# Attention scores of 12 units made in the first six steps, kept in DRAM and fetched later

## Chip, core and metric

The kernel runs on one core of a Trainium2 chip. The metric is the device time of one execution in microseconds, the median of several runs. Engines are called as the profile calls them: PE (TensorE, matmuls), PEld (its weight loads), DVE (VectorE), ACT (ScalarE), POOL (GpSimd) and SP (SyncE, which here issues every DMA).

## What is computed

A top-k attention feeds a two-layer block. There are 8 batches of 8 heads, 576 positions and 64 dimensions a head; every row of scores keeps its 32 largest values.

```python
scores = (1 / sqrt(64)) * q @ k.T                    # 8 x 8 x 576 x 576
kth    = the 32nd largest of each row
scores = where(scores >= kth, scores, -1e9)
attn   = exp(scores - max); attn = attn / (sum(attn) + 1e-9)
x      = (attn @ v), heads side by side              # 4608 tokens x 512
h      = x @ w_in                                    # 512 -> 2048
out    = maximum(0.01 * h, h) @ w_out                # 2048 -> 512
```

All of it is float32.

## The kernel before

**Start.** Sixteen pieces of the weights are loaded and rounded (`round_weights`, L114), with the staging of raw bits in three `raw` buffers. Loads of q and k for the first head pairs, of v, and the scores of units 0 and 1 (`first_scores`, L229) stand between the last pieces (L501 to L517).

**Units and steps.** The attention is cut into 144 units. A whole unit is 128 query rows of one pair of heads, so 2 x 128 rows of 576 scores; a left unit joins the 64 remaining rows of two pairs. The main loop (L540) makes one step for each unit, and every step touches several units at once. At step s:

- DVE finds the top 32 of unit s (`top_k`, L244): a maximum and a minimum of the two halves of each row (L251), then four rounds of MAX8 (L256) with MATCH_REPLACE8 (L259) between.
- POOL masks unit s-1 (`mask`, L263), ACT takes its exponents (L273) and writes the sums to `ze` (L278).
- For unit s-2 DVE takes the reciprocal `rz` of `ze` (L282), ACT normalizes (L285) and splits the words into halves (`split`, L294), SP writes the halves to DRAM (`apart`, L295) and reads them back transposed as `wT` (L299). The units of HASTY are transposed on PE instead (L309, L315).
- PE weighs the values of two units together (`weigh_values`, L336). From unit 14 on this stands at the end of an even step, three steps after the odd unit of the two; the units of HURRIED come one step sooner. ACT copies the result to `x` (L350).
- At even s PE makes the scores of units s+2 and s+3 (`scores`, L203, matmuls L220), and ACT copies them from PSUM to `s_sb` (L227). `s_sb` has five buffers, taken in the order in which units are scored.

**The two layers.** Tokens are handled in 19 chunks: two of 128, then 17 of 256. A chunk is ready once its values are there. Its matmuls are L392 (first layer, `ph`, into `gT` by ACT at L398) and L404 (second layer, `pz`, copied by ACT at L413); the first two chunks go by L360, L365 and L377. They are cut into small pieces, which `mlp_steps` deals out over seven places in each step: `slot_budget` spreads the cost of what is ready until the next chunk will be ready. Scores and values do not count in that budget.

**What sets the order.** The program's order is written out by hand (`tc.manual_schedule`), and each engine goes through its own instructions in that order; an instruction that waits holds up all behind it on its engine. SP does the same with the DMAs. `load_more` (L489) loads v and q with k of later pairs at the end of a step. Eight pairs' q and k fit: five in `qt` and `kt`, three in the `raw` buffers that the weights no longer need.

```python
last = {p: n for n, u in enumerate(steps) for p in u.pairs}
while len(of) < NPAIR and (len(of) < n or last[len(of) - n] + lag <= s):
    load(len(of))
```

Of the kernel before, what the change touches and what calls it, by code (L numbers as in the profile page):

```python
# [9 lines left out]
F32 = mybir.dt.float32  # L10
# [10 lines left out]
def kernel(  # L21
# [41 lines left out]
    work = ctx.enter_context(tc.tile_pool(name="work", bufs=2))  # L63
    small = ctx.enter_context(tc.tile_pool(name="small", bufs=5))
    halves = ctx.enter_context(tc.tile_pool(name="halves", bufs=3, space=bass.MemoryType.DRAM))
    ps_sc = ctx.enter_context(tc.tile_pool(name="ps_sc", bufs=1, space=bass.MemoryType.PSUM))
    ps_ml = ctx.enter_context(tc.tile_pool(name="ps_ml", bufs=2, space=bass.MemoryType.PSUM))

# [31 lines left out]
    def load_weights(n):  # L100
        if n >= NPIECE:
            return
        if not AS_WORDS:
            nc.sync.dma_start(piece(n), weights[n])
            return
        raw_of[n] = raws.tile([P, WCH, 4], U16, name="raw")
        flat = raw_of[n].rearrange("p n w -> p (n w)")
        for m, c0, c1 in ROUNDED:
            if m == n:
                nc.sync.dma_start(flat[:, 4 * c0:4 * c1], weights[n][:, 4 * c0:4 * c1])  # L110
# [92 lines left out]
    def scores(us):  # L203


        narrow = ps_sc.tile([P, 2, 512], F32, name="narrow")
        ps = {}
        for k, u in enumerate(us):
            wide = ps_sc.tile([P, 2, 512], F32, name="wide", bufs=2)
            ps[u] = ((wide[:, :, 0:WIDE], 0, WIDE),  # L210
                     (narrow[:, :, k * NARROW:(k + 1) * NARROW], WIDE, S))

        order = ((us[0], 0), (us[0], 1), (us[1], 1), (us[1], 0))
        for u, part in order:
            to, k0, k1 = ps[u][part]
            for n in range(0, len(u.parts), 2):
                for i, pi, side, r0 in u.parts[n:n + 2]:
                    qt, kt = qk_of[pi]
                    d = slice(side * D, (side + 1) * D)
                    nc.tensor.matmul(to[r0:r0 + u.rows, i, :], qt[d, u.q0:u.q0 + u.rows],  # L220
                                     kt[d, k0:k1], start=True, stop=True)
        for u in us:
            u.both = work.tile([P, 2, S], F32, name="s_sb", bufs=5)
            u.s = [u.both[:, i, :] for i in range(2)]
        for u, part in order:
            to, k0, k1 = ps[u][part]
            nc.scalar.copy(u.both[:, :, k0:k1], to)  # L227

    def first_scores(u):  # L229

        ps = [ps_sc.tile([P, 2, 512], F32, name="wide", bufs=2) for i in range(2)]
        for half in range(2):
            for i, pi, side, r0 in u.parts:
                qt, kt = qk_of[pi]
                d = slice(side * D, (side + 1) * D)
                nc.tensor.matmul(ps[i][:, half, 0:HS], qt[d, u.q0:u.q0 + P],
                                 kt[d, half * HS:(half + 1) * HS], start=True, stop=True)
        yield
        u.both = work.tile([P, 2, S], F32, name="s_sb", bufs=5)
        u.s = [u.both[:, i, :] for i in range(2)]  # L240
        for i in range(2):
            nc.scalar.copy(u.s[i].rearrange("p (h n) -> p h n", h=2), ps[i][:, :, 0:HS])

    def top_k(u):  # L244

# [180 lines left out]
    def mlp_steps(budget):  # L426
        owed[0] += budget
        while owed[0] > 0:
            if running[0] is None:
                if not ready:  # L430
                    owed[0] = 0.0
                    return
                running[0] = mlp(ready.pop(0))
            cost = next(running[0], None)
            if cost is None:
                running[0] = None
            else:
                owed[0] -= cost
                backlog[0] -= cost
# [15 lines left out]

    steps = units

    def unit(n):
        return steps[n] if 0 <= n < len(steps) else None

# [25 lines left out]
    with tc.manual_schedule():  # L486
        last = {p: n for n, u in enumerate(steps) for p in u.pairs}

        def load_more(s):  # L489

            for of, load, n, lag in ((v_of, load_v, LOADED_V, LAG + 1), (qk_of, load_qk, LOADED + 3, 8)):
                while len(of) < NPAIR and (len(of) < n or last[len(of) - n] + lag <= s):
                    load(len(of))
                    if lag > LAG + 1 and len(of) > n:
                        break


        for n in range(3):
            load_weights(n)
        jobs = [round_weights(*job) for job in ROUNDED] if AS_WORDS else [iter(())] * len(ROUNDED)  # L500
        for n in range(len(jobs) + 1):  # L501
            if n == len(jobs) - 1:
                first = first_scores(steps[0])
                next(first, None)
            for job in jobs[max(n - 1, 0):n + 1][::-1]:
                next(job, None)
            if n == len(jobs) - 1:
                next(first, None)
                load_v(0)
                load_v(1)  # L510
            elif n == len(jobs):
                for _ in first_scores(steps[1]):
                    pass
            if n:
                load_weights(n + 2)
            if 0 <= n - len(jobs) + HP + 1 < HP:
                load_qk(n - len(jobs) + HP + 1)  # L517

        def weights_of(u):
            reciprocals(u)  # L520
            normalize(u, 0)
            normalize(u, 1)

        def values(*place):
            due = [u for n, u in enumerate(steps) if values_at(n) == place]
            if due:
                po = ps_sc.tile([P, 2, 512], F32, name="wide", bufs=2)[:, 0, 0:2 * P]
                po = po.rearrange("p (u n) -> p u n", u=2)
            else:
                return ()  # L530
            for n, u in enumerate(due):
                weigh_values(u, po[:, n, :])
            return [(u, po[:, n, :]) for n, u in enumerate(due)]

        def keep(weighed, *place):
            for u, po in weighed:
                keep_values(u, po)
            attended(*place)

        for s in range(len(steps) + LAG + 1):  # L540
            cur, old, older, new = unit(s), unit(s - 1), unit(s - 2), ()
            if s % 2 == 0:
                new = [u for u in steps[s + 2:s + 4] if u]
            picks = top_k(cur) if cur else iter(())
            budget = slot_budget(s)

            def slot():
                next(picks, None)

            at_first = s < HURRY and s - 2 in HURRIED  # L550
            if at_first:
                weights_of(older)
            slot()
            if old:
                mask(old, 0)
                mask(old, 1)
            late = s < HURRY and not {s - 1, s - 2} & set(HURRIED)
            if older and not late and not at_first:
                weights_of(older)
            mlp_steps(budget)  # L560
            weighed = values(s, MIDDLE)
            at_once = s - 2 in HURRIED or any(at == (s, MIDDLE) for at, _ in ready_at)
            if at_once:
                keep(weighed, s, MIDDLE)
            slot()
            if older and late:
                weights_of(older)
            if s - 2 in HASTY:
                transpose_in_haste(older)
            mlp_steps(budget)  # L570
            if old:
                exponents(old, 0)
            mlp_steps(budget)
            if older:
                keep_transposed(older) if s - 2 in HASTY else transpose(older, lambda: mlp_steps(budget))
            if not older or s - 2 in HASTY:
                mlp_steps(budget)
            slot()
            slot()
            mlp_steps(budget)  # L580
            if old:
                exponents(old, 1)
                sums(old)
            mlp_steps(budget)
            if not at_once:
                keep(weighed, s, MIDDLE)
            if new and s < HURRY:
                scores(new)
            keep(values(s, END), s, END)
            if new and s >= HURRY:  # L590
                scores(new)
            budget = slot_budget(s + 1)
            mlp_steps(budget)
            load_more(s)
        mlp_steps(1e9)

# [57 lines left out]
```

## Time and profile before

| what | value |
|---|---|
| median of 6 runs | 1468.27 us (1467.12 to 1468.9) |
| the profiled execution | 1468.9 us |
| its span, first to last instruction | 1467.1 us |
| granted TensorE clock, mean | 0.981 |
| start of step 0 (first L251) | 61.3 us |
| end of the last top-k | about 1381.4 us |
| DMA, all queues | 222.30 MB, mean 152 GB/s |
| DMA q1, share of 16 engines' span | 53.5% |
| apart, 288 KB, issue to landing | 2.1 us |
| kt, 288 KB, issue to landing | 3.7 us |
| wT, issue to landing | 4.6 us |

How to read what follows: in the page, a row of an engine is its busy time, its share of the span and its number of instructions. A row of 40 digits cuts the span in equal slices; a digit is the share in tenths (9 is 90% or more), and PEclk is the clock granted to TensorE. The chain is the work that ended last, followed back from the end, with each engine's share. In a table by stretch a row is start:end and length in us, then busy time and count of PE, PEld, DVE, ACT and POOL, the granted clock, the share of the DMA engines and GB/s. In a timeline a row is start, length, engine, line, operation, out<-in, and in brackets how long the engine had been idle and what ended that. Waits are listed as who waited for whom, with total us, times and longest. One execution is profiled; matmuls are pipelined, and their ends are modelled.

### The profile page before, as it was taken

What the parts mean: (1) busy time and instruction counts of PE and PEld (TensorE: products, weight loads), DVE (VectorE), ACT (ScalarE), POOL (GpSimd) and SP (SyncE); (2) the same over time, 40 slices, a digit from 0 to 9 for tenths busy, and PEclk for the clock granted to TensorE, in tenths of its full rate; (3) what the DMA queues carried; (4) which work ended last, traced back from release to release, by engine and by line L of the source; (5) the groups of instructions that cost most, each with busy time, mean ns of one, the idle gap of its engine ahead of it and who ended that gap; (6) DMA issues with size and microseconds to landing.
All of it is one profiled execution on the core that took longest, in us unless ns stands there. A gap on an engine that the chain in (4) does not pass through costs nothing.

```text
span 1467.1 us, 24106 instructions
## 1 busy us (share of the span) xinstructions
PE 1394.2 (95%) x8066; PEld 927.2 (63%) x8068; DVE 1320.4 (90%) x3401; ACT 1100.8 (75%) x1984; POOL 1096.6 (75%) x744
## 2 busy tenths in 40 slices
PE   7716999999999999999999999999999999999999
PEld 2314548575757676767676767666666666666674
DVE  7999999999999999999999999999999999999600
ACT  8758878777887777777777777777777777777710
POOL 3288888878888888787878788878787878787700
PEclk9958999999999999999999999999999999999999
DMA  9834534654366455664567445655457545554510
GB/s 329 303 85 134 145 105 116 171 153 136 108 196 183 130 138 153 171 185 137 146 166 199 136 137 137 189 171 151 127 160 208 139 136 139 161 139 135 144 49 14
DMA packets 388940, 222.30 MB, mean 152 GB/s; under 512 B 333904, under 2 KB 333904, under 8 KB 386896
## 3 DMA queue, kind: packets, MB, share of 16 engines
q1 hardware_dynamic: 388816, 220.77, 53.5%
q8 instruction: 63, 1.03, 0.3%
q14 instruction: 61, 0.50, 0.1%
HBM read 46.14 MB, written 92.01 MB: 94 GB/s over the span
## 4 chain that ended last, share of the span: by engine, by line
PE 79%; DVE 16%; DMA 2%; ACT 2%; issue 1%; SPq 0%; POOL 0%; DVEq 0%; ACTq 0%; POOLq 0%
PE pz L404 31%; PE ph L392 29%; PE wide L336 10%; DVE tops L256 7%; PE wide L220 6%; DVE pairs L259 5%; PE narrow L220 3%; DVE pairs L251 2%; DMA raw<-in_weights_dram 1%; DVE w_out L155 1%; DVE scale L152 0%; DMA wT<-apart 0%; DVE scale L131 0%; DVE top L133 0%; DMA vt<-in_vk_dram 0%
## 5 line engine op out<-in xcount | busy, mean ns | idle before, releaser
L269 POOL TENSOR_SCALAR pen<-s_sb,tops 128x576 f32<-128x576 f32 x288 | 637.5, 2213 | 210.5 <-DVE tops L256 145.4
L256 DVE MAX8 tops<-pairs 128x8 f32<-128x288 f32 (+1 forms) x1152 | 636.5, 592 | 0.0
L404 PE MATMUL pz<-w_out,gT 128*128 128x512 f32 x1152 | 505.5, 595 | 2.4 <-ACT scale L365 2.4
L392 PE MATMUL ph<-x,w_in 128*128 128x256 f32 x2176 | 482.9, 381 | 0.1
L259 DVE MATCH_REPLACE8 pairs<-tops,pairs 128x288 f32<-128x288 f32 (+1 forms) x864 | 460.6, 539 | 0.0
L392 PEld LDWEIGHTS ph<-x,w_in 128*128 128x128 f32 x2176 | 409.4, 190 | 76.9 <-issue 22.2
L270 POOL TENSOR_TENSOR s_sb<-s_sb,pen 128x576 f32<-128x576 f32 x288 | 406.6, 1412 | 24.1
L404 PEld LDWEIGHTS pz<-w_out,gT 128*128 128x128 f32 x1152 | 216.5, 190 | 267.2 <-issue 262.5
L294 ACT COPY split<-s_sb 128x1152 uint16<-128x1152 uint16 x280 | 309.4, 1146 | 0.0
L285 ACT ACTIVATE s_sb<-s_sb,rz 128x576 f32<-128x576 f32 x288 | 207.6, 773 | 42.6 <-DVE rz L282 42.6
L273 ACT ACTIVATE s_sb<-s_sb,nbias 128x576 f32<-128x576 f32 x288 | 222.3, 772 | 12.8 <-POOL s_sb L270 12.8
L251 DVE TENSOR_TENSOR pairs<-s_sb 128x576 f32<-128x576 f32 x288 | 213.5, 780 | 9.9
L336 PEld LDWEIGHTS wide<-wT,vt 128*64 128x64 f32 x3200 | 161.6, 139 | 68.0 <-issue 34.6
L336 PE MATMUL wide<-wT,vt 128*64 128x128 f32 (+1 forms) x3200 | 179.1, 268 | 25.5 <-ACT s_sb L227 21.8
L227 ACT COPY s_sb<-wide 128x704 f32<-128x704 f32 x142 | 107.1, 754 | 21.8 <-PE wide L220 21.8
L398 ACT ACTIVATE gT<-ph 128x512 f32<-128x512 f32 x136 | 80.7, 593 | 56.3 <-PE ph L392 55.6
L350 ACT COPY x<-wide 128x128 f32<-128x128 f32 (+1 forms) x160 | 32.2, 260 | 113.6 <-PE wide L336 113.6
L220 PE MATMUL wide<-kt,qt 64*128 64x352 f32 (+1 forms) x392 | 75.4, 498 | 26.2 <-ACT s_sb L227 23.0
L413 ACT COPY o_sb<-pz 128x512 f32<-128x512 f32 x36 | 21.1, 585 | 98.4 <-PE pz L404 98.4
L227 ACT COPY s_sb<-narrow 128x448 f32<-128x448 f32 x142 | 68.7, 536 | 0.8 <-PE narrow L220 0.2
L282 DVE RECIPROCAL rz<-ze 128x2 f32<-128x2 f32 x144 | 22.4, 155 | 47.3 <-ACT ze L278 47.2
L259 DVE MATCH_VALUE_LOAD pairs<-tops,pairs 128x8 f32 x864 | 63.4, 73 | 0.0
(61 smaller groups left out, 622.1 us busy)
## 6 DMA issues: line engine op xcount, KB each, us to landing
apart<-split SPq DMA_DIRECT2D x280, 288.0 KB, 2.1
raw<-in_weights_dram SPq DMA_DIRECT2D x15, 1024.0 KB, 7.1
vt<-in_vk_dram SPq DMA_DIRECT2D x32, 320.0 KB, 3.7
out_dram<-o_sb SPq DMA_DIRECT2D x36, 256.0 KB, 2.6
qt<-in_qT_dram SPq DMA_DIRECT2D x20, 288.0 KB, 3.2
kt<-in_kT_dram SPq DMA_DIRECT2D x20, 288.0 KB, 3.7
raw<-in_qT_dram SPq DMA_DIRECT2D x12, 288.0 KB, 3.4
raw<-in_kT_dram SPq DMA_DIRECT2D x12, 288.0 KB, 3.7
```

Source lines behind the costliest of these rows:

```text
L220: nc.tensor.matmul(to[r0:r0 + u.rows, i, :], qt[d, u.q0:u.q0 + u.rows], kt[d, k0:k1], start=True, stop=True)
L251: nc.vector.tensor_tensor(pairs[:, :, n, :], u.both[:, :, 0:HS], u.both[:, :, HS:S], op)
L256: nc.vector.max(out=u.tops[:, i, r, :], in_=rest[i])
L259: nc.vector.match_replace(out=rest[i], in_to_replace=u.tops[:, i, r, :], in_values=rest[i], imm_value=LOWEST)
L269: nc.gpsimd.tensor_scalar(pen, u.s[i], u.tops[:, i, ROUNDS - 1, 7:8], MASKED, ALU.is_lt, ALU.mult)
L270: nc.gpsimd.tensor_tensor(u.s[i], u.s[i], pen, ALU.add)
L273: nc.scalar.activation(u.s[i], u.s[i], AF.Exp, bias=u.nbias[:, i:i + 1], scale=SCALE, accum_out=u.z[:, i:i + 1])
L285: nc.scalar.activation(u.s[i], u.s[i], AF.Copy, bias=0.0, scale=u.rz[:, i:i + 1])
L294: nc.scalar.copy(split, pairs[:, :, h])
L336: nc.tensor.matmul(po[side * D:(side + 1) * D, o, :], vt[:, c, side, :], u.wT[:, c + side * NKC if c + 1 < NKC else c, r:r + n], start=(c ...
L392: nc.tensor.matmul(ph[:, i, 0:n], w_in[c][:, f * P:(f + 1) * P], x[c][:, 0:n], start=(c == 0), stop=(c == HP - 1),)
L404: nc.tensor.matmul(pz[0:m, 0:DMODEL], gT[:, f, r0:r0 + m], w_out[f // 4][:, f % 4, :], start=(f == 0), stop=(f == NFC - 1),)
```

## The change

Twelve whole units get their scores long before their step: 24, 25, 32, 33, then 40, 41, 48, 49, then 56, 57, 64, 65. Each group of four comes from two pairs of heads. While the weights' last pieces are rounded, `load_early` loads the two k and the four pieces of q of each group into one of the three `raw` buffers. At the end of steps 0 to 5, `score_early` makes the scores of 4, 2, 1, 2, 1 and 2 units: PE in two halves of 288 columns, ACT copies them into one of three places in `gT`, which holds no hidden layer yet, and SP writes 576 KB a unit to a DRAM tile of its own. Three steps before its own step, behind the transpose of the step, a unit's scores are fetched into an `s_sb` buffer. The scores of these six pairs at steps 22, 30, 38, 46, 54 and 62 are left out. Pairs 5 to 7 of q and k are loaded at the end of step 5 instead of step 0, as the `raw` buffers are taken until then. At one place HASTY stands for HURRIED.

```diff
+    def load_early(us):
+        raw = raws.tile([P, WCH, 4], U16, name="raw").rearrange("p n w -> p (n w)").bitcast(F32)
+        at = 0
+        for pi in sorted({u.pairs[0] for u in us}):
+            kt = raw[:, at:at + S]
+            nc.sync.dma_start(kt, kT[pi])
+            at += S
+            for u in us:
+                if u.pairs[0] == pi:
+                    early_of[u] = raw[:, at:at + P], kt
+                    nc.sync.dma_start(early_of[u][0], qT[pi][:, u.q0:u.q0 + P])
+                    at += P
+
+    def keep_scores(u):
+        k = len(kept_of)
+        qt, kt = early_of.pop(u)
+        ps = [ps_sc.tile([P, 2, 512], F32, name="wide", bufs=2) if (2 * k + i) % 3 else
+              ps_sc.tile([P, 2, 512], F32, name="narrow") for i in range(2)]
+        for half in range(2):
+            for i, _, side, _ in u.parts:
+                d = slice(side * D, (side + 1) * D)
+                nc.tensor.matmul(ps[i][:, half, 0:HS], qt[d, :], kt[d, half * HS:(half + 1) * HS],
+                                 start=True, stop=True)
+        both = gT.rearrange("p f n -> p (f n)")[:, k % 3 * 2 * S:(k % 3 + 1) * 2 * S]
+        for i in range(2):
+            nc.scalar.copy(both[:, i * S:(i + 1) * S].rearrange("p (h n) -> p h n", h=2), ps[i][:, :, 0:HS])
+        kept_of[u] = kept.tile([P, 2 * S], F32, name=f"kept{k}")
+        nc.sync.dma_start(kept_of[u], both)
+
+    def fetch_scores(u):
+        u.both = work.tile([P, 2, S], F32, name="s_sb", bufs=5)
+        u.s = [u.both[:, i, :] for i in range(2)]
+        nc.sync.dma_start(u.both.rearrange("p i n -> p (i n)"), kept_of[u])
...
+    KEPT = (24, 40, 56)
+    EARLY_SCORES = {0: 4, 1: 2, 2: 1, 3: 2, 4: 1, 5: 2}
...
+                if of is qk_of and to_keep:
+                    while len(of) < LOADED:
+                        load(len(of))
+                    continue
...
+            if n >= len(jobs) - 2:
+                load_early(to_load.pop(0))
             if 0 <= n - len(jobs) + HP + 1 < HP:
                 load_qk(n - len(jobs) + HP + 1)
...
-            at_once = s - 2 in HURRIED or any(at == (s, MIDDLE) for at, _ in ready_at)
+            at_once = s - 2 in HASTY or any(at == (s, MIDDLE) for at, _ in ready_at)
...
+            if unit(s + 3) in early_units:
+                fetch_scores(unit(s + 3))
             slot()
             slot()
...
+            if new and new[0] in early_units:
+                new = ()
             if new and s < HURRY:
                 scores(new)
             keep(values(s, END), s, END)
             if new and s >= HURRY:
                 scores(new)
+            score_early(EARLY_SCORES.get(s, 0))
```

## The prediction

> **What bounds the kernel now.** I read the page first: which engines are full, and which work the chain that ended last runs through.
>
> ```profile
> PE 1394.2 (95%) x8066; PEld 927.2 (63%) x8068; DVE 1320.4 (90%) x3401; ACT 1100.8 (75%) x1984; POOL 1096.6 (75%) x744
> ...
> PEclk9958999999999999999999999999999999999999
> ...
> PE 79%; DVE 16%; DMA 2%; ACT 2%; issue 1%; SPq 0%; POOL 0%; DVEq 0%; ACTq 0%; POOLq 0%
> ```
>
> Two engines are nearly full, and the chain changes between them, so an average says little. The chain in order of time is DVE from 61 to about 190 us, PE to about 375, DVE from 384 to 457, and PE from 463 to the end. I cut the span at starts of steps: L251 starts step 0 at 61.3 us, step 16 at 203.0, step 36 at 387.2 and step 48 at 493.6, and DVE's top-k is over at 1381.4. The table by stretch gives busy time of PE, PEld, DVE, ACT, POOL:
>
> ```profile
> 61.30:203.00 141.70, 90.04 (x519) 51.61 (x518) 140.52 (x368) 102.17 (x188) 112.99 (x77) 0.81 0.45 126
> 203.00:387.20 184.20, 183.11 (x1150) 125.22 (x1149) 176.38 (x460) 140.65 (x271) 149.66 (x101) 1.00 0.47 131
> 387.20:493.60 106.40, 105.21 (x620) 74.80 (x619) 105.55 (x277) 87.04 (x160) 89.81 (x61) 1.00 0.63 174
> 493.60:1381.40 887.80, 886.45 (x5318) 606.11 (x5317) 848.42 (x2208) 699.96 (x1284) 718.33 (x481) 1.00 0.57 154
> 1381.40:1467.10 85.70, 82.03 (x323) 49.97 (x322) 0.33 (x2) 17.21 (x30) 6.74 (x4) 1.00 0.18 51
> ```
>
> In the first stretch DVE is full and PE is idle for 51.7 us. In steps 36 to 47 twelve steps take 106.4 us, 8.87 each, with DVE full: that is DVE's floor, and PE is barely behind. In the second and fourth stretches PE is full and DVE is not. After 1381.4 only PE has work. The waits, asked for by stretch (221 to 387, 387 to 494, 494 to 1382; total, times, longest), show how the two are coupled:
>
> ```profile
> DVE rz L282 <- ACT ze L278: 6.2, 5, 2.5
> ```
> ```profile
> PE wide L336 <- DMA wT<-apart: 1.1, 2, 0.7
> ```
> ```profile
> DVE rz L282 <- ACT ze L278: 33.0, 39, 1.9
> ```
>
> Where PE is late, ACT waits in its fixed order for PE's scores and hidden layers, writes ze late, and DVE stalls at its reciprocal. Where DVE is the floor, PE waits for wT. So a PE microsecond is worth one where DVE still has stalls to give back (6.2 us in stretch two, 33.0 in four), and nothing in steps 36 to 44.
>
> **What is removed.** Six pairs of scores leave steps 22, 30, 38, 46, 54 and 62. One pair in PE's timeline:
>
> ```profile
> 268.29 0.86 PE L220 MATMUL wide<-kt,qt 64*128 64x352 f32 x4
> 268.99 0.54 PE L220 MATMUL narrow<-kt,qt 64*128 64x224 f32 x4
> 269.37 0.55 PE L220 MATMUL narrow<-raw 64*128 64x224 f32 x4
> 269.74 0.76 PE L220 MATMUL wide<-raw 64*128 64x352 f32 x4
> 270.43 0.70 PE L404 MATMUL pz<-w_out,gT 128*128 128x512 f32 x1
> ```
>
> From 268.29 to 270.43 is 2.14 us; the next work follows without a gap. Six pairs make 12.8 us. ACT also loses the pair's four copies (2 x 0.755 + 2 x 0.535 = 2.6 us), which only helps it to catch up. The order of all other instructions on PE, ACT, DVE and POOL is the same in both builds; the new tokens become ready at steps 42, 50, 58 and 66, so in the steps emptied PE goes straight on with hidden-layer work it already has.
>
> Now by stretch. Steps 22 and 30: 4.3 us; DVE's 20 steps there take 184.2 against a floor of 177.3, so 6.9 can be given back: it all passes. Step 38: PE already waits for wT at steps 40 and 42, so these 2.14 become more waiting: 0. Steps 46, 54, 62: 6.4 us. Eight steps take 73.8 us in steady state (L251 at 1141.4 and 1215.2), with one pair less 71.7, still over DVE's 70.9; so PE stays the bound, though with 0.8 us to spare. Counting 33.5 us from DVE's start of an odd unit to its landed wT (units 37 to 41, where nothing else delays it), wT would be there 1.3 us or more before PE at each even step from 48 to 68. Sum: 5 x 2.14 = 10.7 us.
>
> A rule of the Trainium skill speaks against this: "Perfetto Trace Analysis", section "Identifying the Most-Contended Engine", says that matmul occupancy is no measure of TensorE's headroom, and to use the busy share of the weight loads. By that, 63%, PE has a third to spare and the removal is worth nothing. The row says otherwise: from 494 to 1382 us PE waits 1.4 us for others. It is not at its peak rate, but its queue never empties, and a shorter queue ends sooner. I go by the row.
>
> **What is added early.** Twelve units at four matmul groups of 288 columns: 1.24 us each (L236), 14.9 us of PE. PE is idle for 38 of the 53 us of steps 0 to 5, and the granted clock there falls to 0.50. At half clock it is 30 us, which still fits. Value: 0 by either.
>
> ACT copies each unit in 1.17 us (L242, two copies). This must fit the gaps in which ACT waits for DVE's rz, the value before "<-DVE rz":
>
> ```profile
> 92.44 1.44 ACT L285 ACTIVATE s_sb<-s_sb,rz 128x576 f32<-128x576 f32 x2 [1.41 <-DVE rz L282]
> ...
> 101.30 1.44 ACT L285 ACTIVATE s_sb<-s_sb,rz 128x576 f32<-128x576 f32 x2 [3.56 <-DVE rz L282]
> ...
> 110.17 1.44 ACT L285 ACTIVATE s_sb<-s_sb,rz 128x576 f32<-128x576 f32 x2 [1.42 <-DVE rz L282]
> ```
>
> One unit follows each of steps 2 and 4 (gaps of 1.41 and 1.42) and two follow steps 1, 3 and 5 (gaps of 5.46, 3.56 and 3.24 against 2.34); the four after step 0 have 7.7 us. It fits. If it did not, DVE would still have some 3.5 us, as ze is written 97.54 to 97.74 and rz read at about 101.1. Queued behind the copies on ACT are normalize, exponents and splits, whose results are due two steps later. Between 0 and, with every copy twice as dear, 14 - 3.5 = 10 us; I take 0, as the copies are the same shape as L242.
>
> SP gets 18 loads at the start (2.5 MB), 12 writes of 576 KB, and six q and k loads moved from step 0 to step 5. Behind the first six loads stand qk of pair 3, due at 62 us, issued at 50.4 before: 0.85 MB at the 329 GB/s of the first slice is 2.6 us, so it lands by about 58. Behind the moved loads stands the apart of step 6, whose wT landed at 130.0 and is used at 145.1. Pairs 4 to 7 are first read at step 16. The staging in gT is free again by step 6; the first gT write (L377) is at 138.9. All 0 while DVE is the bound, up to step 16; uncovered, a few us at most.
>
> The twelve fetches (576 KB) each stand behind the transpose of the same step on SP and wait only for DVE to have read the buffer's earlier unit two steps before, which is past. They have over two steps (17 us) to land; 1024 KB landed in 7.1 us at the start, so 4.0 by size, and 7.4 as two kt loads of 3.7. Ahead of apart of the next step they cost SP some 0.6 us. What could hurt is the odd-step transpose just ahead: wT of unit 43 landed at 483.54 and PE read it at 483.65. Bounds: below nothing is excluded, as added traffic frees none; above, the whole 1.8 us of 590 KB at 329 GB/s for six odd steps. The nearest row is unit 22's transpose, issued at 284.59 with two loads at 287.90 and 288.52 close behind: it landed 2.04 us after its issue ended, and that of unit 20, with nothing behind it for 3 us, in 2.07. I take 0. The HASTY edit adds step 16 alone, where no values are due: 0.
>
> **The rivals.** (1) All six pairs pay, if step 38 shortens what follows: 12.8, 1455.5. Against it are PE's waits at 40 and 42. (2) DVE and the latency of wT take the bound over between steps 46 and 66, where only 0.8 us per eight steps is left, and two or three pairs pay: 4.3 to 6.4, 1461.9 to 1464.0. (3) No change: fetches overlap the six odd transposes in full, 6 x 1.8 = 10.8 eats the gain. (4) Slower: a fetch holds the transpose ahead of it for the whole time of its own landing, 4.0 to 7.4 us, less some 0.9 of margin, six times: 19 to 39 lost, 8 to 28 net, 1476 to 1497. It decides from 10.7 / 6 + 0.9 = 2.7 us of delay per transpose. Unit 22's speaks against it.
>
> **How the numbers follow.** The profiled execution took 1468.9 us with a span of 1467.1; 10.7 less is 1458.2, and 1457.6 from the median of 1468.27, which I give. Five pairs: 0.55, own range 1456 to 1459.3. Six: 0.12. Two or three: 0.18. No change: 0.07. Slower: 0.08. 0.2% is 2.9 us, about what a measurement here can tell from none, so faster 0.85, same 0.07, slower 0.08. The range takes in the first three cases.
>
> **What would show it.** Right: steps 0 to 15 keep DVE's pace (step 16 near 203), step 36 starts about 4.3 us sooner, step 48 no further ahead than that, and by step 72 it is 10.7; PE waits some 2 us more for wT at steps 40 to 44; wT lands in 4.6 us as before. Wrong: DVE stalls at rz before step 16; wT at 6 us or more behind fetches; new PE waits for wT in steps 46 to 68; or step 36 not earlier, which would mean that the stalls of steps 27 to 35 were not PE's.

## The result and the profile after

The changed kernel takes 1471.63 us (median of 17 runs, 1469.92 to 1474.98), the kernel before 1468.13 us (38 runs, 1466.04 to 1471.23). The ratio is 1.0024, 95% interval 1.0018 to 1.003: 0.24% slower, where 1457.6 us was forecast. The profiled execution took 1469.92 us with a span of 1468.0, the lowest of the 17, so what its trace shows is the mildest case.

First the page of the changed kernel: the rows of the engines, the clock and the chain, and then the group of the values (busy time, mean ns of one | idle time before it and what ended it). Line numbers have moved with the change: scores are now L221 (L220 before), the start of a top-k L292 (L251), `ze` L319 (L278), `rz` L323 (L282), the split L335 (L294), `apart` L336 (L295), the transposes L340 (L299), the values L377 (L336) and the second layer L445 (L404); L175 loads v, and L283 is a fetch. In some of the runs below they are a few higher again.

```profile
PE 1407.0 (96%) x8066; PEld 934.2 (64%) x8068; DVE 1321.7 (90%) x3401; ACT 1101.0 (75%) x1984; POOL 1097.3 (75%) x744
...
PEclk9968999999999999999999999999999999999999
...
PE 75%; DVE 14%; DMA 5%; ACT 4%; issue 1%; SPq 0%; POOL 0%; DVEq 0%; ACTq 0%; POOLq 0%
...
L377 PE MATMUL wide<-wT,vt 128*64 128x128 f32 (+1 forms) x3200 | 179.7, 268 | 15.6 <-DMA wT<-apart 10.0
```

The chain has moved in part from PE and DVE to DMA and ACT: DMA 5% instead of 2%, ACT 4% instead of 2%. The values (L377) wait 10.0 us for the transposed words `wT`. Queue q1 is busy 58.2% instead of 53.5%. These waits are few, so a share of busy time hides them, and the stretches show them. The cuts are at the same steps as before (0, 16, 36, 48, end of the top-k); the columns are busy time of PE, PEld, DVE, ACT and POOL, then granted clock, DMA share and GB/s.

```profile
61.50:204.40 142.90, 112.17 (x620) 64.67 (x618) 140.67 (x368) 116.30 (x213) 113.01 (x77) 0.87 0.66 197
204.40:385.50 181.10, 177.80 (x1114) 121.60 (x1113) 176.25 (x460) 135.76 (x263) 149.60 (x101) 1.00 0.53 146
385.50:494.10 108.60, 103.72 (x590) 74.11 (x590) 105.83 (x276) 83.77 (x153) 89.70 (x61) 0.97 0.70 187
494.10:1382.20 888.10, 883.02 (x5284) 603.93 (x5283) 849.34 (x2208) 694.20 (x1276) 719.25 (x481) 1.00 0.59 157
1382.20:1468.00 85.80, 81.99 (x323) 49.95 (x321) 0.33 (x2) 17.19 (x30) 6.70 (x4) 1.00 0.18 50
```

Lengths against before: +1.2, -3.1, +2.2, +0.3, +0.1 us. Only the second stretch, with the pairs of steps 22 and 30 gone, is shorter. In the fourth, three pairs are gone and nothing is gained. The waits, by step, name the place. PE waits for `wT` in the stretch of steps 36 to 47 and again after step 48:

```profile
PE wide L377 <- DMA wT<-apart: 4.9, 1, 4.9
```
```profile
PE wide L377 <- DMA wT<-apart: 4.5, 2, 3.9
```

The long ones are one wait of 4.9 us in step 41 and one of 3.9 us in step 65. Both are at the values of an odd unit (37 and 61) whose `apart`, like that of the even unit ahead of it, was issued close behind a fetch. Here is SP's queue in the changed kernel ahead of the first of them (start, length, engine, line, operation):

```profile
415.65 2.66 SPq L340 DMA_TRANSPOSE wT<-apart  x1
418.37 0.57 SPq L283 DMA_DIRECT2D s_sb<-kept  x1
418.99 0.42 SPq L175 DMA_DIRECT2D vt<-in_vk_dram  x1
419.51 0.85 SPq L336 DMA_DIRECT2D apart<-split  x2
425.80 2.57 SPq L340 DMA_TRANSPOSE wT<-apart  x1
```

A step's transpose waits for the landing of its two `apart`, and all else on SP waits behind it. The `apart` issued at 419.51 is queued behind a fetch (576 KB) and a load of v (320 KB). The times of its two copies from issue to landing (min, median, max):

```profile
DMA to landing us min/median/max: 5.5/5.6/5.8
```

In the same step before, no load stood close ahead of `apart`, and both copies took 2.1 us:

```profile
421.89 1.38 SPq L295 DMA_DIRECT2D apart<-split  x2
425.10 2.64 SPq L299 DMA_TRANSPOSE wT<-apart  x1
```
```profile
DMA to landing us min/median/max: 2.1/2.1/2.1
```

The changed kernel's `apart` of the step ahead (410.13), also behind a fetch and a load of v but 1.0 us after the load, took 4.8 and 4.4. From 418.40 to 425.80 the DMA engines are busy for 0.94 of the time; in the same wait before, from 421.90 to 425.10, for 0.48. How much later `wT` becomes by this is seen below, against the same kernel without fetches.

### The profile page after: what moved, and what is told of

Read it like the earlier page. It is cut to its first block, busy times and chain, and to the rows that moved or that the text cites. A ratio compares the mean times of both kernels' runs of the same rounds, so it can differ in the third digit from the quotient of the medians.

```text
span 1468.0 us, 24218 instructions
## 1 busy us (share of the span) xinstructions
PE 1407.0 (96%) x8066; PEld 934.2 (64%) x8068; DVE 1321.7 (90%) x3401; ACT 1101.0 (75%) x1984; POOL 1097.3 (75%) x744
## 3 DMA queue, kind: packets, MB, share of 16 engines
q1 hardware_dynamic: 394864, 237.48, 58.2%
## 4 chain that ended last, share of the span: by engine, by line
PE 75%; DVE 14%; DMA 5%; ACT 4%; issue 1%; SPq 0%; POOL 0%; DVEq 0%; ACTq 0%; POOLq 0%
PE pz L445 29%; PE ph L433 28%; PE wide L377 9%; DVE tops L297 6%; PE wide L221 5%; DVE pairs L300 4%; PE narrow L221 3%; DMA apart<-split 2%; ACT split L335 1%; DMA wT<-apart 1%; DVE pairs L292 1%; DMA raw<-in_weights_dram 1%; ACT s_sb L314 1%; ACT s_sb L326 1%; DVE w_out L156 1%
## 5 line engine op out<-in xcount | busy, mean ns | idle before, releaser
L445 PE MATMUL pz<-w_out,gT 128*128 128x512 f32 x1152 | 504.7, 594 | 2.4 <-ACT scale L406 2.4
L445 PEld LDWEIGHTS pz<-w_out,gT 128*128 128x128 f32 x1152 | 216.4, 190 | 266.2 <-issue 261.4
L335 ACT COPY split<-s_sb 128x1152 uint16<-128x1152 uint16 x280 | 309.4, 1146 | 3.3 <-DMA apart<-split 3.3
L292 DVE TENSOR_TENSOR pairs<-s_sb 128x576 f32<-128x576 f32 x288 | 214.8, 785 | 11.0 <-ACT s_sb L228 1.7
L377 PEld LDWEIGHTS wide<-wT,vt 128*64 128x64 f32 x3200 | 161.3, 139 | 58.8 <-issue 36.2
L377 PE MATMUL wide<-wT,vt 128*64 128x128 f32 (+1 forms) x3200 | 179.7, 268 | 15.6 <-DMA wT<-apart 10.0
L228 ACT COPY s_sb<-wide 128x704 f32<-128x704 f32 x130 | 98.0, 754 | 20.7 <-PE wide L221 20.7
L221 PE MATMUL wide<-kt,qt 64*128 64x352 f32 (+1 forms) x360 | 70.0, 501 | 1.0 <-ACT s_sb L243 0.7
L228 ACT COPY s_sb<-narrow 128x448 f32<-128x448 f32 x130 | 62.9, 536 | 1.7 <-PE narrow L221 1.1
L323 DVE RECIPROCAL rz<-ze 128x2 f32<-128x2 f32 x144 | 22.3, 155 | 45.5 <-ACT ze L319 45.5
```

Of the source, the lines that this page charges most:

```text
L292: nc.vector.tensor_tensor(pairs[:, :, n, :], u.both[:, :, 0:HS], u.both[:, :, HS:S], op)
L335: nc.scalar.copy(split, pairs[:, :, h])
L377: nc.tensor.matmul(po[side * D:(side + 1) * D, o, :], vt[:, c, side, :], u.wT[:, c + side * NKC if c + 1 < NKC else c, r:r + n], start=(c ...
L445: nc.tensor.matmul(pz[0:m, 0:DMODEL], gT[:, f, r0:r0 + m], w_out[f // 4][:, f % 4, :], start=(f == 0), stop=(f == NFC - 1),)
```

## The experiments

Each run is compared with the kernel before, timed beside it (median 1468.27 us for e1 to e4, 1468.39 for e5 to e8, 1467.82 for e9 to e11). Theory A: a fetch shares the DMA engines with `apart`, so `wT` is late and PE waits. Theory B: DVE and the latency of `wT` would bound the kernel anyway, and the fetches cost nothing. Theory C: the early work costs the gain.

| run | what differs | us, median | ratio to before |
|---|---|---|---|
| e1_no_fetch | the change without fetches | 1457.72 | 0.9925 [0.9912, 0.9938] |
| e2_early_only | early work only | 1469.36 | 1.0007 [0.9998, 1.0015] |
| e3_odd_fetch | both fetches at odd steps | 1465.22 | 0.9976 [0.9967, 0.9985] |
| e4_skip_only | before, without six pairs | 1460.38 | 0.9944 [0.993, 0.9958] |
| e5_act_queue | fetches issued by ACT | 1473.95 | 1.004 [1.0027, 1.0054] |
| e6_odd_steps | even units alone fetched | 1462.09 | 0.9957 [0.9945, 0.9969] |
| e7_even_steps | odd units alone fetched | 1460.65 | 0.9951 [0.994, 0.9963] |
| e8_loads_later | no loads in steps of a fetch | 1465.94 | 0.9983 [0.9973, 0.9992] |
| e9_free_steps | other units fetched, loads spread | 1458.93 | 0.9942 [0.9929, 0.9954] |
| e10_free_steps_only | other units fetched | 1460.50 | 0.9946 [0.9932, 0.9959] |
| e11_spread_only | loads spread | 1473.21 | 1.0038 [1.0026, 1.0051] |

**Gain and cost apart: e1, e2, e4.** In e1 the changed kernel loses its fetches; ACT copies columns of a weight into the score buffers instead, so those 12 units are worked on other data.

```diff
-            if unit(s + 3) in early_units:
-                fetch_scores(unit(s + 3))
...
+            nc.scalar.copy(u.both.rearrange("p i n -> p (i n)"), w_in[k][:, 0:2 * S])
```

> The changed kernel without its twelve fetches: the early scores, their copies and their writes to DRAM stay, the scores of the six later pairs stay left out, and where they stood ACT copies columns of the weights into s_sb (so these twelve units work on other data; PE saves the same 2.14 us a pair, ACT does about the same copying as before the change). Theory A (the 576 KB fetches stand ahead of the apart of the next step in the DMA queue, so wT lands late and PE waits): the gain comes back almost whole, 1458 to 1461 us, step 36 starts some 4 us sooner than in the kernel before, and PE's waits for wT in steps 40 to 66 fall from 9 us to at most 3. Theory B (DVE and the latency of wT bound these steps whatever PE does): 1464 to 1470, waits for wT stay. Theory C (the early work costs what the later steps gain): 1466 to 1471, with step 16 late.

It took 1457.72 us. Its steps start earlier than before by 4.2 us at 36, 4.2 at 48 and 10.6 at 72, and 10.7 at 143. So the change without fetches is worth the sum that was forecast, and the fetches cost 1471.63 - 1457.72 = 13.9 us. B falls. PE in e1 waits for `wT` once in the whole main loop:

```profile
PE wide L383 <- DMA wT<-apart: 1.9, 1, 1.9
```

(and once 1.1 us for v). This wait is in step 40. Its transposes show what the fetches do to SP's sequence. Those of units 34, 37, 59 and 61, first in e1 and then in the changed kernel:

```profile
393.14 2.30 SPq L346 DMA_TRANSPOSE wT<-apart  x1
...
420.29 2.45 SPq L346 DMA_TRANSPOSE wT<-apart  x1
...
618.51 2.64 SPq L346 DMA_TRANSPOSE wT<-apart  x1
...
636.36 2.32 SPq L346 DMA_TRANSPOSE wT<-apart  x1
```
```profile
395.60 2.46 SPq L340 DMA_TRANSPOSE wT<-apart  x1
...
625.00 2.74 SPq L340 DMA_TRANSPOSE wT<-apart  x1
...
647.19 2.57 SPq L340 DMA_TRANSPOSE wT<-apart  x1
```

From unit 34 to unit 37 e1 takes 27.2 us, and the changed kernel 30.2 (its transpose of unit 37 is the one at 425.80 above). From unit 59 to 61 e1 takes 17.9 us, and the changed kernel 22.2. So `wT` loses 3.0 us in three steps before the wait of step 41, and 4.3 in two before that of step 65.

In e2 the scores are made early and written, but neither fetched nor left out later:

```diff
-            if unit(s + 3) in early_units:
-                fetch_scores(unit(s + 3))
...
-            if new and new[0] in early_units:
-                new = ()
```

> The changed kernel with the early loads, scores, copies and writes, but no fetch and no scores left out: all pairs are scored at their step as before the change. The sum of it is the price of the early work alone. Theory A: 1.2 us at step 8 (ACT's ze late, as in the changed kernel's profile) and little else, 1468 to 1470 us. Theory B: the same. Theory C: 1472 or more.

It took 1469.36, 1.1 us over before, with an interval that just includes no difference. One new wait is in its trace, in step 8, and the steps after it start 0.7 to 1.3 us late to the end. C falls: 1.1 is not 13.9. The wait of step 8 is the same in the changed kernel. SP issues two writes of early scores at 122.21, the six moved loads of q and k from 123.27 to 127.75, and then two `apart`. SP's queue, ACT and DVE of the changed kernel from there:

```profile
127.85 0.85 SPq L336 DMA_DIRECT2D apart<-split  x2
134.88 2.43 SPq L340 DMA_TRANSPOSE wT<-apart  x1
```
```profile
134.20 1.15 ACT L335 COPY split<-s_sb 128x1152 uint16<-128x1152 uint16 x1 [0.75 <-DMA apart<-split]
```
```profile
137.92 0.17 DVE L323 RECIPROCAL rz<-ze 128x2 f32<-128x2 f32 x1 [1.05 <-ACT ze L319]
```

Behind two writes and six loads `apart` landed only after 6.3 and 6.5 us. ACT's next split needs that buffer, ACT stands 0.75 us, everything behind it on ACT comes late, `ze` among it, and DVE, the bound there, loses 1.05 us. But the loads are not the whole cause. ACT was late before it waited for `apart`: it comes 1.3 us late to the gap behind step 4, waits there for PE's early scores, copies them, and normalizes at 113.02 instead of 110.17, which is 2.6 us late counted from step 0.

```profile
111.95 0.64 ACT L276 COPY gT<-narrow 128x576 f32<-128x576 f32 x1 [1.73 <-PE wide L272]
...
113.02 1.45 ACT L326 ACTIVATE s_sb<-s_sb,rz 128x576 f32<-128x576 f32 x2
```

At its copy to `x` (130.93, before at 129.30) it is still 1.4 us late. In e9 and e11 below, where these loads are spread over three steps, ACT waits for no `apart` before step 16, and DVE loses 1.3 and 1.2 us at the same reciprocal all the same. e11's:

```profile
138.23 0.17 DVE L323 RECIPROCAL rz<-ze 128x2 f32<-128x2 f32 x1 [1.22 <-ACT ze L319]
```

In e4 the kernel before leaves six pairs' scores out, with the same copies in their place, and has no early work:

```diff
+            skipped = new if new and new[0] in left_out else ()
+            if skipped:
+                new = ()
...
+            stand_in(skipped)
```

> The kernel before with only the scores' matmuls of the six pairs left out; ACT copies columns of the weights into s_sb in their place (these twelve units work on other data). No early work, no fetch, loads as before. Theory A: the prediction's sum of 10.7 us, less what ACT's copies now cost without PE, 1457 to 1460 us. Theory B: 2 to 6 us at most, 1462 to 1466. Theory C: as A, 1457 to 1460.

It took 1460.38, a gain of 7.9 us. Its profiled span was 1457.1 us, 10.0 less than before; that execution took 1460.89 us, so 3.8 us lie outside the span. In three of its six executions 2.8 to 3.8 us do, in the other three, and in all of e1, 1.7 to 1.8. Its steps start 5.1 us earlier at 36, 11.2 at 72 and 10.0 at 143. By span the removal is worth some 10 us again. That this kernel's median is 2.7 us over e1's, with less work, is not explained.

**Which fetches: e6, e7, e3.** Fetches were forecast to be dangerous only where a transpose for an odd unit, used at once, stands ahead of one; theory A at first gave the harm to the fetches at even steps, ahead of the `apart` of the odd step. In e6 only the fetches at odd steps are left, in e7 only those at even steps; the other six units again get a copy of a weight.

```diff
-                fetch_scores(unit(s + 3))
+                (fetch_scores if s % 2 == 1 else stand_in)(unit(s + 3))
```

(`s % 2 == 0` in e7.)

> Of each pair only the even unit is fetched (at odd steps); for the odd unit ACT copies columns of the weights into s_sb at the place of its fetch, so these six units work on other data. Theory A (the harm is the fetch ahead of an odd unit's apart, so that of the even steps): 1458 to 1462 us. If the odd-step fetches held the transposes ahead of them, as the prediction's slower rival had it: 1466 to 1471.

> The other half: only the odd unit is fetched (at even steps), the even unit's scores are replaced by ACT's copy of weights. Theory A: nearly all the loss stays, 1466 to 1471 us. The prediction's slower rival: 1458 to 1462.

e6 took 1462.09 us and e7 1460.65. Against e1 the odd ones cost 4.4 us and the even ones 2.9; theory A had expected 1466 to 1471 for e7. Neither kind is the harmful one, and 4.4 + 2.9 = 7.3 is about half of 13.9. PE's waits for `wT` from 300 to 720 us, e6 and then e7:

```profile
PE wide L382 <- DMA wT<-apart: 5.3, 3, 3.0
```
```profile
PE wide L382 <- DMA wT<-apart: 3.1, 3, 2.3
```

In the changed kernel they sum to 9.3 us between the same times. The lateness of SP's sequence, counted as above, explains this. From unit 34 to unit 37, e6 is 1.1 us slower than e1, as 1.5 of the 2.7 us that its one fetch cost come back in the step without one; e7 is 0.3 slower, and the changed kernel, with a fetch in both steps, 3.0. PE's long wait behind that is 1.9 us in e1, 3.0 in e6, 2.3 in e7 and 4.9 in the changed kernel. From unit 59 to 61 the lateness is 2.5, 1.4 and 4.3 us, and PE, with some slack there, waits 1.7, 0.3 and 3.9 in step 65. So a step without a fetch lets SP catch up, and the slack takes in one fetch better than two. In e3 both fetches of a pair stand at the odd step, so that the even step is free:

```diff
-            if unit(s + 3) in early_units:
+            if s % 2 and unit(s + 3) in early_units:
                 fetch_scores(unit(s + 3))
+            if s % 2 and unit(s + 2) in early_units:
+                fetch_scores(unit(s + 2))
```

> The changed kernel with both fetches of a pair moved to odd steps, behind the transpose of an odd unit: the even unit's at its step less three as before, the odd unit's at its own step less two (one step later than in the change). Then no fetch stands ahead of the apart of an odd unit, whose wT is due soonest. Theory A: most of the loss goes, 1459 to 1464 us, wT of units 37 and 61 lands without the 3 to 6 us wait for apart. Theory B: as the change, 1469 to 1472. If the loss comes from the odd-step fetches holding the transpose ahead of them, as the slower rival of the prediction had it, also 1469 to 1472.

It took 1465.22, a little over the 1459 to 1464 of theory A, and with a new cost: the odd unit's scores now come too late for DVE. Its waits up to 720 us:

```profile
DVE pairs L292 <- DMA s_sb<-kept: 10.8, 4, 4.6
```

The two steps that a fetch was given in the prediction are less on the chip, as SP runs behind DVE. In the changed kernel the transpose of step 37 is issued at 406.06, when DVE has begun step 38 (403.25); the fetch behind it has from 408.55 to the start of step 40 at 420.91, 12.4 us and not 17. In the changed kernel DVE never waits for a fetch; one step less, and it does.

**The queue or the DMA engines: e5.** If the order on SP's queue were the cause, another queue would cure it. In e5 ACT issues the fetches.

```diff
-        nc.sync.dma_start(u.both.rearrange("p i n -> p (i n)"), kept_of[u])
+        nc.scalar.dma_start(u.both.rearrange("p i n -> p (i n)"), kept_of[u])
```

> The changed kernel with the fetches issued by ACT instead of SP, at the same place in the program: the bytes are the same, but they no longer stand in SP's queue ahead of apart. Theory A1 (order in one queue is the cost: apart lands only after all that was issued ahead of it): most of the 13.9 us that the fetches cost comes back, 1459 to 1464 us. Theory A2 (the DMA engines' time is the cost, whichever queue issues): as the change, 1469 to 1473, apart of the next step as late as with SP.

It was no faster: 1473.95, with an interval that overlaps that of the change. The `apart` beside a fetch that has no load near it; SP's row, ACT's, and the landing of those `apart`:

```profile
564.25 1.01 SPq L336 DMA_DIRECT2D apart<-split  x2
```
```profile
564.41 0.33 ACTq L283 DMA_DIRECT2D s_sb<-kept  x1
```
```profile
DMA to landing us min/median/max: 5.5/5.6/5.7
```

From another queue, and issued 0.16 us later than the first `apart`, the fetch makes `apart` as slow as ahead of it on SP. So the order in one queue is not what delays it. The Trainium skill names what all queues share ("DMA: Bandwidth & Descriptors", section "Issuing engines are not separate DMA queues": DMAs of all issuers run on the same 16 engines and interleave), and these rows and the busy share of 0.94 above agree; no run here tells the DMA engines from the DRAM behind them. ACT pays for the issuing in e5 (0.33 to 0.37 us each time), so its time as a whole does not price the queue alone.

**The loads beside the fetches: e8, e11, e9, e10.** In e8 the loads of v, q and k leave the steps with a fetch:

```diff
+            if s > 30 and unit(s + 3) in early_units:
+                return
```

> The changed kernel with the loads of v, q and k at the ends of steps 37, 38, 45, 46, 53, 54, 61 and 62 put off until the next step without a fetch; all else as in the change (it computes what the reference computes). Theory A says that a fetch hurts most where loads join it ahead of apart (PE's longest waits, 4.9 us at step 41 and 3.9 at step 65, are where 320 KB of v and 576 KB of q and k stand with it): 1463 to 1467 us. If 576 KB alone fill the gap, or the put-off loads do the same harm one step later: 1468 to 1472.

1465.94, 5.7 us better than the change. The wait at step 65 is gone. In step 40 three loads of v now come together, `apart` takes 6.1 to 6.2 us there, and PE waits 2.4 us in step 40 and 2.5 in step 43, together as long as it did in step 41. In e11 the loads are spread, one pair a step, but the fetches stay:

```diff
-                    if lag > LAG + 1 and len(of) > n:
+                    if lag > LAG + 1 and len(of) > LOADED:
```

> The change with the twelve units it has, but q and k of pairs 5, 6 and 7 loaded one pair at a step from step 5 on. Theory A: only the stall at step 8 goes (1.1 us), the fetches cost what they did: 1469.5 to 1471.5 us.

1473.21, no better: a load of v (420.68) still stands beside the fetch of 420.05, the `apart` behind them takes 5.5 to 5.7 us, and PE waits 5.2 us in step 41 much as it did. It is over the 1469.5 to 1471.5 that were expected, but its interval overlaps that of the change. The stall of step 8, which was to go, stays, as shown above. In e9 six other pairs of units are fetched, each in two steps that no load falls in and where PE is the bound, and the loads are spread:

```diff
-    KEPT = (24, 40, 56)
+    KEPT = (56, 72, 86, 104, 120, 134)
-        to_keep = [[steps[n] for n in (a, a + 1, a + 8, a + 9)] for a in KEPT]
+        to_keep = [[steps[n] for n in (a, a + 1)] for a in KEPT]
-                if len(to_keep) % 4 == 0 and to_load:
+                if len(to_keep) % 2 == 0 and to_load:
-                    if lag > LAG + 1 and len(of) > n:
+                    if lag > LAG + 1 and len(of) > LOADED:
```

> The change with other twelve units and with its moved loads spread. Kept are the pairs 56, 72, 86, 104, 120 and 134 with their next unit, so the fetches stand at steps 53/54, 69/70, 83/84, 101/102, 117/118 and 131/132, in none of which v, q or k are loaded, and all lie where PE is the bound; q and k of pairs 5, 6 and 7 are loaded one pair at a step from step 5 on. Theory A (a fetch hurts by sharing the DMA engines with apart and loads, and PE's time is worth its own length where PE is the bound): six pairs of 2.14 us pay, 12.8, less at most 2: 1455 to 1458 us, no wait for wT over 1 us near a fetch, step 8 without its stall. If 576 KB in each of two steps running already hold apart too long: 1461 to 1466.

1458.93 us, 0.58% faster than before, with all scores computed: it beats both kernels, and is 0.9 us over what was expected. e10 has the same units and the loads as in the change:

> The same other twelve units, but the three pairs of q and k all loaded at the end of step 5 as in the change. Theory A: the sum of the run with both, plus the 1.1 us that the early work cost: 1456 to 1459 us, with ACT's late ze at step 8. If the early stall is made up where PE is the bound: no difference.

1460.50, 1.5 us over what was expected; its interval and e9's overlap. So the choice of units does nearly all of it, and spreading the moved loads little or nothing. In e9 the `apart` beside a fetch still takes more than twice its time; the landing of those from 556 to 567 us, and all waits of PE for `wT` after 494 us:

```profile
DMA to landing us min/median/max: 4.5/4.6/5.0
```
```profile
PE wide L377 <- DMA wT<-apart: 3.5, 4, 2.5
```

What differs from the change is that no load stands beside the fetches, and that no pair of scores is taken out where DVE is the bound; e9 does not tell the two apart. That the first counts is shown by e8, where moving loads alone gained 5.7 us. PE waits 0.4 us in steps 103 and 105 and 2.5 us in step 121; behind the other fetches it waits 0.2 us at most. That 2.5 is over the 1 us that was expected at most near a fetch. Six pairs of 2.14 us less the 3.5 us of waits would be 9.3 us; 8.9 were measured.

## Why the prediction was wrong

**PE as the bound, and 5 x 2.14 us: right in mechanism and sum, in part by luck.** e1 shows the marks that were set: step 36 earlier by 4.2 us (4.3 forecast), step 48 no further ahead, step 72 by 10.6 (10.7). At step 40 PE waits 1.9 us; that is 0.8 more than the 1.1 of steps 40 and 42 before, where some 2 were forecast, and 1.6 more go into slower matmuls behind the wait. The skill's rule on occupancy, read as the prediction read it (by the weight loads; the page names MFU, the share of the peak rate, beside them, which was not worked out here), would have given nothing, and these runs speak against that reading. The luck is in the 4.2 at step 36, a net figure: e1 was 1.6 us late at step 16, so 5.8 us were gained between, not 4.3. e9, where nothing is left out before step 54, lost 1.5 us by step 24 and had 1.2 of them back by step 28, so a late start is partly given back by DVE's stalls there. But e4, only 0.7 us late at step 16, gains 5.8 us between too. So two pairs gave more than 2 x 2.14 us there, and the loss of the early work hid it; why they gave more is open.

**Fetches at 0: this step failed, and it turns the sign.** The working asked how long a fetch takes (4.0 to 7.4 us; 5.0 measured) and what it does to the transpose ahead of it (nothing; those with a fetch close behind, issued at 406.06 and 415.65, landed in 4.4 and 4.7 us, so that the sign "wT at 6 us or more behind fetches" never came). Of the `apart` that follows it said "Ahead of apart of the next step they cost SP some 0.6 us". That is the price of the issue alone. `apart` shares the DMA engines with the fetch and the load beside it, and takes 4.4 to 5.8 us instead of 2.1 in steps 37 and 38, 5.7 to 6.3 in 61 and 62. Against e1 each such step adds 1.0 to 2.3 us of lateness to SP's sequence, and two in a row use up the 1.3 us or more by which `wT` was forecast to land before PE. Of the signs set for being wrong, new waits for `wT` in steps 46 to 68 came, and DVE's stall before step 16. In step 40 or 41 PE waits 1.9 us in e1, as the forecast had it for the pair of step 38, and 4.9 in the changed kernel: the 3.0 lost by SP come on top. In step 65 e1 doesn't wait, and the changed kernel waits 3.9, of 4.3 lost. After the wait PE is slow as well. The changed kernel's PE around step 41:

```profile
430.46 2.40 PE L377 MATMUL wide<-wT,vt 128*64 128x128 f32 x20 [4.88 <-DMA wT<-apart]
432.79 1.55 PE L221 MATMUL wide<-kt,qt 64*128 64x352 f32 x4
...
436.06 9.28 PE L445 MATMUL pz<-w_out,gT 128*128 128x512 f32 x21
```

and by window, the granted clock in the third column from the end:

```profile
430.40:433.00 2.60, 2.54 (x22) 2.21 (x24) 2.60 (x10) 0.09 (x1) 2.46 (x2) 0.50 0.85 331
433.00:436.00 3.00, 3.00 (x16) 2.01 (x16) 3.00 (x10) 1.50 (x4) 2.87 (x2) 0.65 0.25 52
```

Twenty such matmuls took 1.31 us before:

```profile
428.09 1.31 PE L336 MATMUL wide<-wT,vt 128*64 128x128 f32 x20
```

Here they take 2.40, and the pair of scores 436.06 - 432.79 = 3.27 instead of 2.14. The wait of 4.88 costs 4.88 + 1.09 + 1.13 = 7.1 us of PE. In step 65 the same sum is 3.93 + 0.31 + 1.32 = 5.6:

```profile
652.71 1.62 PE L377 MATMUL wide<-wT,vt 128*64 128x128 f32 x20 [3.93 <-DMA wT<-apart]
654.27 1.55 PE L221 MATMUL wide<-raw 64*128 64x352 f32 x4
...
657.73 2.84 PE L445 MATMUL pz<-w_out,gT 128*128 128x512 f32 x6
```

With four shorter waits for v and `wT` (1.44, 0.64, 0.52 and 0.63) PE loses 15.9 us to late data; e1 loses 1.1 + 1.9 and, in matmuls slowed in the same way, 1.6: 4.6. The difference is 11.3 us, and the two spans differ by 1468.0 - 1456.4 = 11.6. By the medians it is 13.9, as the changed kernel's profiled execution was its quickest and e1's its slowest.

Where PE is late, ACT and DVE follow: the second wait comes back at DVE as 1.65 us for scores and 2.04 us for `ze` in step 66:

```profile
657.83 2.64 DVE L292 TENSOR_TENSOR pairs<-s_sb 128x576 f32<-128x576 f32 x2 [1.65 <-ACT s_sb L228]
...
664.09 0.17 DVE L323 RECIPROCAL rz<-ze 128x2 f32<-128x2 f32 x1 [2.04 <-ACT ze L319]
```

**Early work at 0: a small miss.** It cost 1.05 us in step 8 (1.1 us by e2), and two terms were off. ACT did not have the room that was counted: the gap of 1.42 us behind step 4 was filled with a copy of 1.17, but ACT also waits there 1.73 us for PE, and normalizes 2.6 us late. And the moved loads were priced by the slack of one `wT` (130.0, used at 145.1); ACT's split, which waits for the buffer behind the same `apart`, was not asked about, and took 0.75 us. e9 and e11 show that without that wait the stall is no smaller, so the shares of the two are open.

**The rivals.** The slower one, at 0.08, had the sign and a wrong place: it held the transpose, not `apart`. Its 19 to 39 us were too much. The second rival, DVE and the latency as the bound without any help of the fetches, is excluded by e1. The third, in which overlap with the transposes eats the gain, came nearest in time, by another transfer.

Left open: why e4 has up to 2 us more outside its span in half of its executions, why the stall of step 8 survives without the bunched loads, and how e9's gain divides between steps without loads and pairs taken out where PE is the bound.

## What to carry to other kernels

A transfer costs more than its own landing: ask which short transfer on a path of dependent steps lands beside it on the same DMA engines, how far that one is stretched, and whether the path has a step in which to catch up before the next. Price gain and cost by separate runs, with stand-in data for the one and unused work for the other; here they were 10.6 and 13.9 us, and the difference alone would have told neither. Twelve fetches of the same size were worth having in e9 and e10, where no other load stands in their steps and PE, the engine that was relieved, is the bound.

## What the hardware showed

`apart`, two copies of 288 KB, from issue to landing: 2.1 us alone; 3.8 to 4.0 with a load of 320 KB just ahead; 3.4 to 5.0 with a fetch of 576 KB (e8, e9); 4.4 to 5.8 with both; 5.7 to 6.3 with a fetch and 576 KB of q and k; 6.3 and 6.5 behind two writes and six loads. In these runs it grows with the bytes that are under way, and the closer behind them it is issued: in e8, 1.4 us after a fetch it took 3.4 to 3.7, and 0.6 us after one 4.3 to 5.0. In e5 a fetch issued by ACT, on another queue, stretched it too (5.5 to 5.7).

A wait of PE can cost 0.4 to 0.9 of its own length again in slow matmuls (2.2 us after 4.88, 1.6 after 3.93, 1.6 after 1.85), and the length of the wait does not tell it. After 4.88 us the granted clock was 0.50 and then 0.65, some 5.6 us in all. In e1 a wait of 1.85 us was followed by 0.53, and twenty matmuls of the values took 2.29 us. In e9 a wait of 2.52 us was followed by full speed, 1.31 us for the same twenty. e1, then e9:

```profile
424.97 2.29 PE L383 MATMUL wide<-wT,vt 128*64 128x128 f32 x20 [1.85 <-DMA wT<-apart]
```
```profile
424.97:427.20 2.23, 2.23 (x22) 1.90 (x22) 2.23 (x5) 2.22 (x4) 1.11 (x3) 0.53 0.72 277
```
```profile
1163.38 1.31 PE L377 MATMUL wide<-wT,vt 128*64 128x128 f32 x20 [2.52 <-DMA wT<-apart]
```
```profile
1163.38:1166.00 2.62, 2.62 (x32) 2.24 (x34) 2.62 (x10) 0.90 (x3) 2.44 (x3) 1.00 0.26 98
```

The Trainium skill gives an idle window of about 3.4 us as what lowers the clock ("TensorE: Matmul & The Clock Gate", section "What's actually happening"); the wait in e1 was shorter than that and lowered it all the same.
